# Normalising A through DRAM and GpSimd, and k's transpose ahead of C's, in a fused Nystromformer and GLU kernel

## Chip, cores, metric

One core of one Trainium2 chip. The metric is the device time of that core in microseconds (us), the median of several executions. Most executions of one kernel lie within 0.3 to 1.5% of each other; a few fall in a slower state at a lower granted TensorE clock and are left out of ratios, but not of medians. "TensorE" and PE are the same engine, so are VectorE and DVE, ScalarE and ACT, GpSimd and POOL, SyncE and SP.

## The reference, cut

```python
# q, k, v: [8 batches, 8 heads, 576, 64] fp32; m = 32 landmarks (means over 18 rows)
def sm(a, b): ...                       # softmax(scale * a @ b.T) over the last axis
A  = sm(q, k_lm)                        # 576 x 32
Bm = sm(q_lm, k_lm)                     # 32 x 32
C  = sm(q_lm, k)                        # 32 x 576
Z  = Bm.T / (norm_1(Bm) * norm_inf(Bm) + 1e-6)
for _ in range(6): Z = 2*Z - Z @ Bm @ Z
attn = A @ Z @ C @ v
x   = attn as [4608, 512]
out = (sigmoid(x @ w_gate) * (x @ w_val)) @ w_out      # d_ff = 1536
```

## The kernel before

The program lays eight batches over each other. It carries a small model of the chip and a scheduler: every step says which data it needs, the model says when they will be there, and the scheduler emits instructions in that planned time. The order on each engine is fixed when the kernel is built; on the chip an engine takes its instructions in that order and waits wherever data are not there yet. The last stage of the FFN (`op`) serves as filler while other data are awaited. Names that recur below: `sa`, `sl` and `bs` are the scores for A, C and B; `sm` the row sums of A; `ct` is C transposed and `cv` the product C V; `n`, `s` and `pn` are matmuls on the way to Z; `gp` and `vp` are the FFN's gate and value products, which VectorE joins to `ht` (a "gate"), and `op` is the output product, copied out to `ob`.

How the model plans DMA, from which the order follows:

```python
def turn(self, src, dst):               # DMA transpose
    start = max(self.free["pe"], self.free["sp"], self.landed.get(src.name, 0.0))
    busy = 0.026 * elements / 2048
    self.free["sp"] = start + busy
    end = self.free["sp"] + (3.0 if self.free["dma"] > start else 2.5)
    ...                                 # landed[dst] = end
def swap(self, src, dst):               # the small copies of s4, below
    ...
    end = max(self.free["sp"], self.free["dma"]) + 2.5
SLACK, LAG, FILL = 0.02, 20, 1.0        # of the scheduler: how far it fills ahead, and so on
```

Front of a batch: k and q are turned by DMA, GpSimd sums them to landmarks, halves are exchanged by DMA, and `klm`, `bq` come out.

```python
for what in ("k", "q") if b >= TURN else ():            # TURN = 3
    ...
    turned[what] = turn(t, ..., n, ...)                 # kT, qT on the SP queue
for what in ("k", "q"):
    ...
    pool.tensor_add(out=s1, in0=t[:, :, 0:P6], in1=t[:, :, P6:2 * P6])       # 768 columns
    pool.tensor_add(out=s2, in0=s1, in1=t[:, :, 2 * P6:3 * P6])              # 768 columns
    if b >= SWAP and what == "k" and b < B - 1:         # SWAP = 3
        load(b + 1, "k"); load(b + 1, "q")
    pool.tensor_add(out=s3, ...); pool.tensor_add(out=s4, ...)               # 256 columns each
...                                                     # s4 halves swapped by DMA on SP
pool.tensor_add(out=klm, in0=hls["k"], in1=other["k"])
for c in range(2):
    pool.tensor_add(out=bq[r, :, m * c:m * c + m], in0=hls["q"][r], in1=other["q"][r])
```

Middle of a batch: scores for C (`sl`) and B (`bs`) need `bq`; C's rows `cl` are turned by DMA to `ct`; `cv` = C V follows. DVE spreads B into block diagonals, each product with two sources in SBUF.

```python
ct = sb.tile([128, 2 * NC, 128], BF16, name=f"ct_{b}", tag="ct", bufs=1)
turn(ct, ct, cl, cl.rearrange("p g c x -> p (g c x)"))
turned_c[b] = ()
...
dve.tensor_mul(out=dst[:, g], in0=blk, in1=src[...])    # bdT from Bt, later bd from Bc
ce = dve.tensor_scalar_add(out=ce, in0=cc, scalar1=1e-6)
def late_value():
    yield need(ct, v_landed[0], banks=1, tile='cv')     # 48 small matmuls cv <- vn, ct
```

A's normalisation, and which front may start:

```python
def norm(b):                    # per batch: 10 sm, DVE reciprocal and split, rtp,
    ...                         # 10 rb, and 4 products on DVE
    an = sb.tile([128, 2, S], BF16, name=f"an_{b}", tag="an", bufs=3)
    dve.tensor_mul(out=an[:, g, n0:n0 + nn], in0=aexp[:, g, n0:n0 + nn], in1=rb)
def fronts():
    for b in range(B):
        yield ... made(mid_of, b - 2)
        if b > TURN: yield made(turned_c, b - 1)        # C's transpose first
        yield from front(b)
```

The softmax here doesn't subtract the row's maximum and nothing guards it: scores larger than these inputs give would overflow.

## Time and profile before

| | before |
|---|---|
| time, median | 271.88 us (271.79 to 272.63) |
| span in the trace | 269.7 us |
| busy: PE, DVE, ACT, POOL | 260.1, 193.3, 159.4, 96.2 us |
| granted TensorE clock | 0.998 |

The lines on TensorE are shown in the prediction. The SP queue around 120 us (start, time to issue, what): C's transpose goes out ahead of k's.

```profile
DMA to landing us min/median/max: 3.8/4.6/5.1
```

DVE spreads B (`bdT`, two instructions, 0.36 us) at 121.5; GpSimd's first sum of k for batch 5 begins at 126.9, well after it.

```profile
121.53 0.36 DVE L153 TENSOR_TENSOR bdT<-blk,Bt 128x128 bf16<-128x128 bf16 x2
```
```profile
126.92 1.64 POOL L153 TENSOR_TENSOR s_5k<-kT 128x768 f32<-128x768 bf16 x1 [11.31 <-DMA kT<-kn]
```

### The profile page before, as it was taken

The numbers are of one execution on the slowest core, as the hardware profiler recorded it, in microseconds if no ns is written. First come the engines' busy times: TensorE is split into PE (matmuls) and PEld (weight loads), VectorE is DVE, ScalarE is ACT, GpSimd is POOL, SyncE is SP. The second block draws the span as 40 slices with busy tenths as digits, with TensorE's granted clock in tenths as the row PEclk, the third lists the DMA queues.
The fourth block names the chain that finished last, engine by engine and source line by source line (L and its number), as shares of the span: only waits on it lengthen the run. The fifth ranks groups of instructions, "written<-read, shape, count | busy, mean of one in ns | idle before, by whom it ended". The sixth has DMA issues, their size and how long they took to land.

```text
span 269.7 us, 8019 instructions
## 1 busy us (share of the span) xinstructions
PE 260.1 (96%) x3089; PEld 167.0 (62%) x3123; DVE 193.3 (72%) x551; ACT 159.4 (59%) x413; POOL 96.2 (36%) x107
## 2 busy tenths in 40 slices
PE   8999999999999999999999999999999999999994
PEld 5877777757664666556646665556636664665443
DVE  4566888976899788948986778848968786963111
ACT  3663876866647754876477655875368643964001
POOL 8523231960874039511953078212922000000000
PEclk9999999999999999999999999999999999999999
DMA  6999999999795998889794989589530413101433
GB/s 94 193 206 205 205 206 206 205 203 172 141 194 115 204 170 121 181 135 199 141 221 72 182 157 203 129 139 199 124 90 12 97 41 80 41 0 41 117 103 92
DMA packets 62645, 38.00 MB, mean 141 GB/s; under 512 B 33552, under 2 KB 58128, under 8 KB 62608
## 3 DMA queue, kind: packets, MB, share of 16 engines
q0 software_dynamic: 23600, 18.88, 47.0%
q1 hardware_dynamic: 38896, 18.52, 31.4%
q8 instruction: 24, 0.39, 0.6%
q14 instruction: 13, 0.11, 0.1%
q10 hardware_dynamic: 112, 0.10, 0.1%
HBM read 37.75 MB, written 9.44 MB: 175 GB/s over the span
## 4 chain that ended last, share of the span: by engine, by line
PE 93%; ACT 2%; issue 2%; POOL 1%; DVE 0%; POOLq 0%; ACTq 0%
PE op L247 34%; PE gp L247 18%; PE vp L247 18%; PE idle_ps L247 3%; PE pn L247 2%; PE cv L247 2%; PE rb L247 2%; PE sc L247 1%; PE sa L247 1%; PE tp_q L252 1%; PE up_1g L247 1%; PE up_0g L247 1%; PE up_2g L247 1%; PE tp_k L252 1%; PE up_1v L247 1%
## 5 line engine op out<-in xcount | busy, mean ns | idle before, releaser
L247 PE MATMUL op<-wo_sb,ht 128*128 128x512 bf16 (+1 forms) x410 | 109.4, 373 | 2.1 <-issue 1.1
L153 ACT ACTIVATE th<-gp 128x288 bf16<-128x288 f32 x192 | 76.7, 415 | 48.4 <-PE gp L247 36.7
L153 DVE SCALAR_TENSOR_TENSOR ht<-th,vp 128x288 bf16<-128x288 bf16 x192 | 82.0, 448 | 21.9 <-ACT th L153 17.2
L247 PE MATMUL gp<-an,U 128*128 128x288 bf16 x384 | 78.5, 286 | 0.3
L247 PE MATMUL vp<-an,V 128*128 128x288 bf16 x384 | 78.4, 286 | 0.0
L247 PEld LDWEIGHTS <-ht 128*128 128x128 bf16 x444 | 39.9, 98 | 26.7 <-issue 5.8
L247 PEld LDWEIGHTS <-U 128*128 128x128 bf16 x384 | 35.9, 98 | 27.3 <-issue 2.5
L247 PEld LDWEIGHTS <-V 128*128 128x128 bf16 x384 | 37.5, 98 | 9.7 <-issue 0.2
L153 ACT ACTIVATE ob<-op 128x512 f32<-128x512 f32 (+1 forms) x31 | 18.2, 587 | 29.6 <-PE op L247 24.2
L153 DVE SCALAR_TENSOR_TENSOR sy<-sy,pn 128x384 bf16<-128x384 bf16 x35 | 19.2, 548 | 2.3 <-PE pn L247 1.9
L153 DVE TENSOR_SCALAR ob<-op 128x512 f32<-128x512 f32 (+2 forms) x7 | 4.2, 596 | 17.3 <-PE op L247 17.3
L247 PE MATMUL idle_ps<-idle_w 128*128 128x256 bf16 x86 | 14.8, 308 | 1.2 <-DVE idle_w L297 1.2
L247 PE MATMUL pn<-sy 128*128 128x192 bf16 (+1 forms) x84 | 13.1, 237 | 0.4 <-ACT kT L153 0.3
L153 DVE TENSOR_TENSOR an<-aexp,rb 128x384 bf16<-128x384 bf16 (+1 forms) x32 | 12.4, 446 | 0.3 <-PE rb L247 0.3
L247 PEld LDWEIGHTS <-sy 128*128 128x128 bf16 x88 | 8.1, 97 | 6.2 <-DVE sy L153 2.8
L153 ACT ACTIVATE aexp<-sa 128x288 bf16<-128x288 f32 x32 | 10.7, 418 | 1.5 <-PE sa L247 1.1
L247 PEld LDWEIGHTS <-idle_w 128*128 128x128 bf16 x86 | 8.5, 109 | 3.3 <-DVE idle_w L297 1.2
L247 PEld LDWEIGHTS <-WT 64*32 64x32 bf16 x384 | 3.8, 89 | 9.1 <-issue 6.6
L270 POOL DMA_DIRECT2D kn<-in_k_dram x9 | 7.0, 779 | 4.6 <-DMA wg_sb<-in_moe_w_gate_dram 2.1
L153 DVE CAST U<-up_0g 128x512 bf16<-128x512 f32 x8 | 5.5, 690 | 4.1 <-PE up_0g L247 4.1
L270 POOL DMA_DIRECT2D vn<-in_v_dram x8 | 6.3, 789 | 5.3 <-PE gp L247 4.5
L270 POOL DMA_DIRECT2D qn<-in_q_dram x9 | 6.8, 753 | 4.0 <-PE sm L247 2.2
(201 smaller groups left out, 349.7 us busy)
## 6 DMA issues: line engine op xcount, KB each, us to landing
vn<-in_v_dram POOLq DMA_DIRECT2D x8, 576.0 KB, 9.4
kn<-in_k_dram POOLq DMA_DIRECT2D x7, 576.0 KB, 8.1
qn<-in_q_dram POOLq DMA_DIRECT2D x7, 576.0 KB, 10.6
out_dram<-ob SPq DMA_DIRECT2D x53, 64.0 KB, 3.0
out_dram<-ob SPq DMA_DIRECT2D x17, 192.0 KB, 2.3
out_dram<-ob SPq DMA_DIRECT2D x18, 128.0 KB, 2.4
wg_sb<-in_moe_w_gate_dram POOLq DMA_DIRECT2D x3, 512.0 KB, 19.7
wv_sb<-in_moe_w_val_dram POOLq DMA_DIRECT2D x3, 512.0 KB, 21.0
```

Of the source, the lines that this page charges most:

```text
L153: f(**kw)
L247: nc.tensor.matmul(**kw)
L252: nc.tensor.transpose(**kw)
L270: nc.gpsimd.dma_start(out=t[:, hs], in_=src[b, hs].rearrange("h (p c) d -> p h (c d)", p=P6))
```

## The change

Intent: take matmuls from TensorE and products from DVE. **W**: for batches 3 to 6 the row sums of A come from 8 tiled matmuls, DVE takes reciprocals, they are written to DRAM and read back by four broadcast reads issued behind each other, and GpSimd multiplies A in place. **K**: from batch 4 on, k's transpose and sums go ahead of C's transpose, so that GpSimd has done them before the products come; for this the fronts start by another rule, and the loads of the next k and q are issued later. **Rest**: products are made in place (`aexp` has three buffers, `an` goes away, the last `y` has one buffer).

```diff
+    def widen(self, src, dst, n=1):                    # the model's plan of write and reads
+        start = max(self.free["pe"], self.free["sp"], self.landed.get(src.name, 0.0), ...)
+        self.free["sp"] = start + 0.5 * n
+        end = self.free["sp"] + 3.2
...
-        for what in ("k", "q") if b >= TURN else ():
+        for what in ("k", "q") if TURN <= b <= SWAP else ():
+            yield from turned_by_dma(what)
         for what in ("k", "q"):
+            if b > SWAP:
+                if what == "q":
+                    yield made(turned_c, b - 1)         # only q waits for C's transpose
+                yield from turned_by_dma(what)
+                if what == "q" and b < B - 1:
+                    load(b + 1, "k")
...
-            if b >= SWAP and what == "k" and b < B - 1:
+            if b == SWAP and what == "k":
                 load(b + 1, "k")
+                load(b + 1, "q")
+            elif b > SWAP and what == "q" and b < B - 1:
                 load(b + 1, "q")
...
-        aexp = sb.tile([128, 2, S], BF16, name=f"aexp_{b}", tag="aexp", bufs=2)
+        aexp = sb.tile([128, 2, S], BF16, name=f"aexp_{b}", tag="aexp", bufs=3)
...
+    def wide_norm(b, aexp):                            # WIDE = 3 <= b < B - 1
+        for c in range(2):
+            for j in range(4):
+                mm(out=sm[32 * j:32 * j + 32, :], lhsT=pairs[0][:, c], rhs=aexp[...], ...)
+        for x in range(2):
+            at = dve.reciprocal(out=ra[:, half], in_=sm[:, half])
+        nc.sync.dma_start(out=far..., in_=ra)
+        for i in range(NP):
+            nc.sync.dma_start(out=wide[32 * i:32 * i + 32],
+                in_=far[:, :, i, 0].rearrange("g w x -> (g w) x").partition_broadcast(32))
+        for j in range(4):
+            pool.tensor_mul(out=part, in0=part, in1=wide[:, j])
...
-        an = sb.tile([128, 2, S], BF16, name=f"an_{b}", tag="an", bufs=3)
+        an = aexp
-            ... name=f"y_{b}_{it + 1}", tag=f"y{last}", bufs=2)
+            ... name=f"y_{b}_{it + 1}", tag=f"y{last}", bufs=1 if last else 2)
...
-            if b > TURN:
+            if TURN < b <= SWAP:
                 yield made(turned_c, b - 1)
             yield from front(b)
```

More of the change, by code (lines that the diff above doesn't have):

```diff
@@ L140, in swap @@
         self.used[src.name] = self.used[dst.name] = self.landed[dst.name] = end
+    def widen(self, src, dst, n=1):
+        start = max(self.free["pe"], self.free["sp"], self.landed.get(src.name, 0.0),
+                    self.waits.get(dst.name, 0.0))
+        self.free["sp"] = start + 0.5 * n
+        end = self.free["sp"] + 3.2
+        self.used[src.name] = self.used[dst.name] = self.landed[dst.name] = end
 class Timed:
@@ L209 @@
     ITERS = 6
-    DEFER = {"bs": 1.0, "sl": 1.0, "sa": 3.0, "cv": 0.5, "up": 0.0}
+    DEFER = {"bs": 1.0, "sl": 1.0, "sa": 3.0, "cv": 0.5, "up": 0.0, "sm": 1.0}
     LEAD, FIRST, ORDER = 100.0, (2,), ('k2', 'q2', 'o0', 'o1', 'o2', 'v2', 'k3', 'q3', 'v3')
@@ L217 @@
     SWAP = 3
+    WIDE, QT, pairs = 3, S // 4, []
     consts = ctx.enter_context(tc.tile_pool(name="consts", bufs=1))
@@ L222 @@
     sb = ctx.enter_context(tc.tile_pool(name="sb", bufs=2))
+    away = ctx.enter_context(tc.tile_pool(name="away", bufs=1, space=bass.MemoryType.DRAM))
     ps = ctx.enter_context(tc.tile_pool(name="ps", bufs=3, space=bass.MemoryType.PSUM))
@@ L410, in front, with turned_by_dma @@
         ends = {}
-        for what in ("k", "q") if b >= TURN else ():
+        def turned_by_dma(what):
             yield made(nat, (what, b))
@@ L716, in mid @@
             value_of[b] = late_value
+    def wide_norm(b, aexp):
+        if b == WIDE:
+            pairs.append(consts.tile([128, 2, 32], BF16, name="pairs"))
+            nc.vector.memset(pairs[0], 0.0)
+            to = pairs[0].rearrange("p c (i u d) -> p c i u d", u=4, d=2)
+            for c in range(2):
+                dve.tensor_copy(out=to[:, c, :, :, c], in_=blk0_[:, :, None].to_broadcast([128, NP, 4]))
+        yield need(aexp, banks=1, tile='sm')
+        sm = bank([128, QT], FP32, f"sm_{b}")
+        for c in range(2):
+            for j in range(4):
+                o = (j % 2) * HF + c * QT
+                mm(
+                    out=sm[32 * j:32 * j + 32, :], lhsT=pairs[0][:, c],
+                    rhs=aexp[:, j // 2, o:o + QT], start=(c == 0), stop=(c == 1))
+        ra = sb.tile([128, QT], FP32, name=f"ra_{b}", tag="ra", bufs=1)
+        for x in range(2):
+            half = slice(x * QT // 2, (x + 1) * QT // 2)
+            at = dve.reciprocal(out=ra[:, half], in_=sm[:, half])
+            yield need(at + (0.3 if x == 0 else 0.0))
+        far = away.tile([2, 2, NP, 4, HF], FP32, name=f"far_{b}", tag="far", bufs=2)
+        nc.sync.dma_start(out=far.rearrange("g w i u (c x) -> (g w i u c) x", c=2), in_=ra)
+        model.widen(ra, far)
+        wide = sb.tile([128, 4, HF], FP32, name=f"rw_{b}", tag="rw", bufs=1)
+        for i in range(NP):
+            nc.sync.dma_start(
+                out=wide[32 * i:32 * i + 32],
+                in_=far[:, :, i, 0].rearrange("g w x -> (g w) x").partition_broadcast(32))
+        model.widen(far, wide, NP)
+        yield need(wide)
+        for j in range(4):
+            part = aexp[:, j // 2, (j % 2) * HF:(j % 2 + 1) * HF]
+            pool.tensor_mul(out=part, in0=part, in1=wide[:, j])
+        an_of[b] = aexp
     def norm(b):
         aexp = norm_of.pop(b)
+        if WIDE <= b < B - 1:
+            yield from wide_norm(b, aexp)
+            return
         yield need(aexp, banks=1)
@@ L783, in first_newton @@
             last = it == ITERS - 1
-            n = sb.tile([128, 2, 2, D] if last else [128, 2, D], BF16, name=f"y_{b}_{it + 1}", tag=f"y{last}", bufs=2)
+            n = sb.tile([128, 2, 2, D] if last else [128, 2, D], BF16, name=f"y_{b}_{it + 1}", tag=f"y{last}", bufs=1 if last else 2)
             model.by_part.add(n.name)
```

## The prediction

> **What bounds the kernel now.** I read the page first: engines, slices, chain.
>
> ```profile
> PE 260.1 (96%) x3089; PEld 167.0 (62%) x3123; DVE 193.3 (72%) x551; ACT 159.4 (59%) x413; POOL 96.2 (36%) x107
> PE   8999999999999999999999999999999999999994
> PEclk9999999999999999999999999999999999999999
> PE 93%; ACT 2%; issue 2%; POOL 1%; DVE 0%; POOLq 0%; ACTq 0%
> ```
>
> TensorE is busy in every slice, at full granted clock, and 93% of the chain that ends last is TensorE itself. Since a pipelined matmul can look busy while it waits, I then read the table of windows for the steady part, where batches 3 to 6 are normalised.
>
> ```profile
> 124.00:130.00 6.00, 5.84 (x108) 4.00 (x108) 4.83 (x18) 3.51 (x10) 3.00 (x2) 1.00 0.99 197
> 130.00:136.00 6.00, 5.95 (x51) 4.03 (x51) 5.77 (x17) 2.41 (x7) 5.83 (x7) 1.00 0.81 127
> 160.00:166.00 6.00, 5.95 (x52) 4.11 (x52) 5.70 (x17) 2.44 (x6) 5.83 (x6) 1.00 0.99 158
> 178.00:184.00 6.00, 5.95 (x43) 3.93 (x42) 3.35 (x14) 4.50 (x18) 0.00 (x0) 1.00 1.25 221
> ```
>
> The columns are the length, then PE, its weight loads, DVE, ACT, POOL, then clock, DMA share and GB/s. PE has 5.84 to 5.95 of 6 us; DVE looks near full where it normalises (5.77), but its records overlap (two gates stand 0.365 us apart though each is recorded as 0.447), so it has room. To see whether PE's busy time is work or disguised waiting, I went through the timeline start by start:
>
> ```profile
> 125.18 0.41 PE L247 MATMUL vp<-an,V 128*128 128x288 bf16 x2
> 125.52 0.44 PE L247 MATMUL sa<-qT,klm 64*32 64x288 bf16 x16
> ...
> 127.47 0.41 PE L247 MATMUL sm<-blk,aexp 128*128 128x4 bf16 x10
> 127.74 0.59 PE L247 MATMUL op<-wo_sb,ht 128*128 128x512 bf16 x2
> ...
> 129.25 0.22 PE L252 MATMUL rtp<-ident,rhl 128*80 128x128 bf16 x1
> 129.31 0.41 PE L247 MATMUL gp<-an,U 128*128 128x288 bf16 x2
> ...
> 130.40 0.68 PE L247 MATMUL rb<-rt,sel 80*128 80x128 bf16 x10
> 130.91 0.60 PE L247 MATMUL op<-wo_sb,ht 128*128 128x512 bf16 x2
> ```
>
> What an instruction costs is the distance to the next start, not its recorded length: a pair of gp is 0.245 us, a pair of op 0.43. When I lay these distances on the built order of matmuls, nothing of weight is left over from batch 3 on: the largest excess between two neighbouring gp is 0.2 us. So PE has no stall there to be freed; only the matmuls themselves can become fewer, and anything that arrives late is a pure loss.
>
> **What the Trainium skill says.** "TensorEngine Tiling (Array Packing)", Tiling Modes, Key Properties: changing the tiling mode drains the array. The trace agrees and gives the size: from vp at 125.18 two matmuls of 0.1225 end at 125.42, sa starts at 125.52; all eleven entries from vp into a tiled group show 0.093 to 0.094 us. "GPSIMD Engine Reference", 3.1 Elementwise: about 2.6 cycles an element for two inputs at 1.2 GHz, 2.17 ns; the trace has 1.64 us for 768 elements, 2.13 ns, so it agrees. "DMA: Bandwidth & Descriptors", Anatomy of one DMA: some 2 us are fixed in each transfer, most of it the receipt; the trace has 1.9 us to landing for 32 KB outputs and 2.3 for 192 KB, so it agrees. "Perfetto Trace Analysis", Identifying the Most-Contended Engine, warns that matmul busy share is no measure of headroom; that is why I counted starts.
>
> **The change, part by part.** All four steps concern batches 3, 4, 5 and 6 only.
>
> 1. Removed on PE, per batch: ten sm matmuls, 0.27 us (127.47 to 127.74); one transpose rtp, 0.07 (56 to 87 ns over the batches); ten rb, 0.51 (130.40 to 130.91). Sum 0.85, four times 3.4 us.
>
> 2. Added on PE, per batch: eight matmuls of 144 columns into four strips of 32 columns. Four strips run beside each other, as in the up groups, where sixteen of 512 columns take about 0.45 us net of drains. So two rounds of 144 columns: 2 x 144/512 x 0.213 = 0.12 us, four times 0.5 us.
>
> 3. Drains. In the built order the changes between tiled and untiled mode rise from 88 to 104. Three of the four new sm groups stand alone (two changes each), the one of batch 5 joins the cv group; the rest comes from groups that used to stand together and are now apart (sa from cv in batches 2, 5 and 7, a split of sl in batch 5, bs from up in batch 1), because the order has shifted. 16 x 0.094 = 1.5 us lost. One more idle matmul at the start: 0.1 us.
>
> Sum on PE: -3.4 + 0.5 + 1.5 + 0.1 = **-1.3 us**. This is the whole gain that can reach the end.
>
> 4. DVE: the four products go away.
>
> ```profile
> L153 DVE TENSOR_TENSOR an<-aexp,rb x32: 344/446/553, 24.2 to 223.0; 128x384 bf16<-128x384 bf16 x16, 128x192 bf16<-128x192 bf16 x16
> L153 DVE RECIPROCAL sm<-sm x8: 405/408/417, 21.9 to 218.9; 128x40 f32<-128x40 f32 x8
> ```
>
> Per batch 4 x 0.446 = 1.8 us, the reciprocal 0.41, two splits of 0.2 and the rt copy 0.2; added are two reciprocals of 72 columns, an estimate of 0.6 us each from 0.41 at 40 columns. So about 1.6 us less a batch, 6 in all. It lies beside PE and is worth nothing directly. GpSimd gets 4 products of 288 elements, 4 x (0.1 + 288 x 2.13 ns) = 2.8 us a batch; it is 36% busy, so this fits in total. Its order is what counts.
>
> 5. The new chain. The old one ran PE, DVE, PE, DVE, PE, DVE in about 5 us (sm at 127.5, last product at about 132.5). The new one: sm, two reciprocals (1.2), a write to DRAM (2.3 to 3), four broadcast reads, issued one behind another at 0.55 each (the two halves of s_4k take 1.1 on the queue) and moving 590 KB at the 200 GB/s the page shows (3 us) plus 2 us fixed, then 2.8 on GpSimd: 12 to 14 us, more where q and k loads share the DMA engines. The built order has put first use of the result far back: laid out by the starts above, sm to first gp grows from 13 to 15 us to 27, 20, 26 and 17 us. PE fills this with op matmuls, which are no extra work. So the chain itself fits in every batch.
>
> 6. k ahead of C's transpose. GpSimd stands idle for k's transpose in every batch:
>
> ```profile
> POOL s_4k L153 <- DMA kT<-kn: 12.9, 1, 12.9
> POOL s_6k L153 <- DMA kT<-kn: 11.5, 1, 11.5
> POOL s_5k L153 <- DMA kT<-kn: 11.3, 1, 11.3
> ```
>
> The change starts it some 10 us earlier and thereby makes room on GpSimd for the products. PE did not wait for these sums, so it gains nothing directly.
>
> **Rivals.**
> (a) A late product stalls PE. For it: in GpSimd's order the products of batch 3 stand behind the sums of kT_5, those of batch 5 behind kT_7. From the transpose's issue it is 5.9 us to landing, then 4.8 us of sums, then 2.2 us to the third product, which the first gp needs: 13 us, and the built order leaves about 15 us between that place and the first gp. Slack is 2 us in batches 3 and 5, 3 or more elsewhere. A wait behind broadcast traffic or output writes could eat it: 0 to 2 us each, which would give 271.5 to 274. Against it: before, the same planner left PE no stall.
> (b) DVE or ACT becomes the bound. Because op tiles are run in advance while the product is awaited, the gp and vp come in denser runs later; each pair of pairs needs a tanh and a gate per 0.49 us of PE, and a gate takes 0.365. Against it: around 203 us the kernel before runs eight such units in a row at 0.488 without a gap, and DVE has 6 us less to do. If it came, 1 to 2 us lost: about 272.5.
> (c) Outputs and swaps are held up on the one queue behind the wait for the DRAM write (some 2.5 us, four times). Output buffers are three and a tile comes every 6 us, so it should hide: no effect.
> (d) The gain is larger, about 268 to 269: it would need a stall before that DVE or GpSimd caused. I found none after batch 3, and the first 60 us are hardly touched.
>
> **Range and chances.** -1.3 on PE, and for (a) and (b) an expected loss of 0.6, gives 271.88 - 0.7, **271.2 us**. Low end: the whole gain and some of (d), 269.6. High end: two stalls of (a) and a bit of (b), 273.4. 2% is 5.4 us: faster would need four times the PE work that is saved net, 0.03; slower needs a stall of nearly 7 us, which only a broadcast far slower than thought could make, 0.04; within 2%, 0.93.
>
> **What would show it.** Busy PE should fall by 2 to 4 us of its records; the new sm groups should stand 0.12 us plus two drains of 0.094 from their neighbours; rb and rtp should number half; DVE busy should fall by some 6 to 8 us, POOL rise by about 11. The waits should show s_5k to s_7k waiting less for kT, and no wait of PE of over 1 us for the products in batches 4 and 6. The read from DRAM should land in 4 to 7 us. I am wrong if PE shows a gap of several us before the first gp of batch 3 or 5, if a product on GpSimd takes well over 0.8 us, or if PE falls by more than 3 us in the span.

## More of the kernel before

```profile
119.13 1.88 SPq L384 DMA_TRANSPOSE ct<-cl  x1
121.11 3.52 SPq L384 DMA_TRANSPOSE kT<-kn  x1
```

The second is the view of the tile `ct`: time from issue to landing of its five transposes.

## The result, and the profile after

Ratios here and below are the mean time of one kernel's fast runs over the mean of the other's in the same rounds, so not quite the ratio of the medians that are quoted.

| | before | after |
|---|---|---|
| median (lowest to highest) | 271.95 us (271.79 to 272.63) | 284.62 us (281.54 to 286.61) |
| ratio | | 1.042, 95% interval 1.034 to 1.051 |
| span of the profiled run, clock | 269.7 us, 0.998 | 279.3 us, 0.991 |

The change makes the kernel slower by 4.2%. The profiled run of the changed kernel is its fastest, 9.7 us behind the kernel before. From its page: engines, PE and clock in 40 slices, and the chain that ended last.

```profile
PE 265.1 (95%) x3072; PEld 164.3 (59%) x3072; DVE 194.6 (70%) x534; ACT 158.6 (57%) x409; POOL 107.0 (38%) x123
PE   7899999999998899987999999998999999999994
PEclk9999999999999999997999999999999999999998
PE 56%; DMA 25%; POOL 9%; DVE 4%; issue 2%; SPq 1%; ACT 1%; POOLq 0%; DVEq 0%; ACTq 0%
```

Slices below 9 have appeared in PE's row, the clock dips, and 25% of the chain are now DMA and 9% GpSimd, where before 93% were TensorE. So TensorE waits. The timeline of PE at the deepest place (start, length, what, how many, and in brackets the idle time and what ended it):

```profile
124.07 0.44 PE L258 MATMUL sa<-qT,klm 64*32 64x288 bf16 x16
127.16 0.56 PE L258 MATMUL cv<-vn,ct 96*32 96x64 bf16 x48 [2.65 <-DMA ct<-cl]
127.65 3.99 PE L258 MATMUL op<-wo_sb,ht 128*128 128x512 bf16 x10
131.57 0.31 PE L258 MATMUL sm<-aexp,pairs 128*32 128x144 bf16 x8
```

TensorE stands 2.65 us for C's transpose of batch 4. Before, the same pair `sa`, `cv` follows without a gap (125.52, then 125.89). The wait costs a second time: the ten `op` after it take 3.92 us to the next start, where ten take 2.15 at 0.215 each. The table of windows tells why; the last numbers are clock, DMA share and GB/s:

```profile
127.70:131.00 3.30, 3.30 (x10) 1.13 (x9) 0.60 (x2) 0.00 (x0) 3.14 (x6) 0.50 0.94 237
```

The granted clock is half. This one place costs 2.65 + 1.8 = 4.4 us. The SP queue shows what was ahead of C's transpose, and the view of the tile `ct` how long its transposes took to land:

```profile
115.66 2.88 SPq L395 DMA_TRANSPOSE kT<-kn  x1
119.15 1.72 SPq L1022 DMA_DIRECT2D out_dram<-ob  x4
121.39 1.57 SPq L395 DMA_TRANSPOSE ct<-cl  x1
```
```profile
DMA to landing us min/median/max: 3.7/5.7/6.1
```

Its source was ready at 118.1 by the trace (the last `cl` ends there); k's transpose and four outputs were ahead of it in the queue, it went out at 121.39 and landed at 127.12. The other transposes land later too: k's took 5.9 us in the median before, 8.7 after.

A second kind of loss stands at 93 to 96 us. DVE, then GpSimd, then PE:

```profile
93.47 0.74 DVE L161 TENSOR_SCALAR ce<-cc 128x2 f32<-128x2 f32 x1
95.05 1.07 DVE L161 TENSOR_TENSOR bd<-blk,Bc 128x128 bf16<-128x128 bf16 x2
```
```profile
92.54 1.64 POOL L161 TENSOR_TENSOR s_4k<-kT 128x768 f32<-128x768 bf16 x1 [6.76 <-DMA kT<-kn]
94.26 1.64 POOL L161 TENSOR_TENSOR s_4k<-s_4k,kT 128x768 f32<-128x768 f32 x1
```
```profile
96.54 0.64 PE L258 MATMUL sa<-qT,klm 64*32 64x288 bf16 x9 [0.70 <-DVE ht L161]
```

`ce` is an addition on two columns, some 0.17 us elsewhere; here it takes 0.74 and ends at 94.21, just after GpSimd's sum of k ends at 94.18. The first of the two `bd` takes 0.94 us in place of 0.22 and ends at 95.98, just after the second sum ends at 95.90. The gates behind them are late, and TensorE waits 0.70 us for one.

TensorE's other waits of over 0.4 us from batch 1 on: 0.84 and 0.46 us for `bq` at 84 to 85, 0.45 for `bq` at 181, about 0.5 for `bdT` at 186 (by the distances of starts), 1.07 for `ct` of batch 6 at 191. With 2.65, 0.70 and the 1.8 of half clock these are 8.5 us, of the 9.6 us by which the spans of the profiled runs differ. Batch 3, where `bq` is awaited at 84 to 85, is one that K does not touch.

### The profile page after: what moved, and what is told of

Read it like the earlier page. It is cut to its first block, busy times and chain, and to the rows that moved or that the text cites. A ratio compares the mean times of both kernels' runs of the same rounds, so it can differ in the third digit from the quotient of the medians.

```text
span 279.3 us, 8001 instructions
## 1 busy us (share of the span) xinstructions
PE 265.1 (95%) x3072; PEld 164.3 (59%) x3072; DVE 194.6 (70%) x534; ACT 158.6 (57%) x409; POOL 107.0 (38%) x123
## 4 chain that ended last, share of the span: by engine, by line
PE 56%; DMA 25%; POOL 9%; DVE 4%; issue 2%; SPq 1%; ACT 1%; POOLq 0%; DVEq 0%; ACTq 0%
PE op L258 21%; PE gp L258 10%; PE vp L258 9%; DMA ct<-cl 4%; DMA qT<-qn 4%; DMA kT<-kn 4%; DMA far<-ra 3%; DMA qn<-in_q_dram 3%; DMA rw<-far 2%; PE idle_ps L258 2%; POOL bq L161 2%; DMA s_6q<-s_6q 2%; POOL s_6q L161 2%; POOL s_3q L161 2%; DMA s_5q<-s_5q 2%
## 5 line engine op out<-in xcount | busy, mean ns | idle before, releaser
L161 DVE SCALAR_TENSOR_TENSOR ht<-th,vp 128x288 bf16<-128x288 bf16 x192 | 81.0, 447 | 10.6 <-ACT th L161 8.1
L258 PE MATMUL gp<-aexp,U 128*128 128x288 bf16 x384 | 78.5, 286 | 0.0
L258 PE MATMUL vp<-aexp,V 128*128 128x288 bf16 x384 | 78.4, 286 | 0.0
L258 PEld LDWEIGHTS <-ht 128*128 128x128 bf16 x444 | 40.5, 99 | 38.0 <-issue 8.7
L161 ACT ACTIVATE ob<-op 128x512 f32<-128x512 f32 (+1 forms) x23 | 13.4, 584 | 32.6 <-PE op L258 29.8
L161 DVE TENSOR_SCALAR ob<-op 128x512 f32<-128x512 f32 (+2 forms) x15 | 9.7, 646 | 30.1 <-PE op L258 30.0
L161 POOL TENSOR_TENSOR aexp<-aexp,rw 128x288 bf16<-128x288 bf16 x16 | 11.2, 736 | 15.5 <-DMA rw<-far 8.4
L161 ACT ACTIVATE aexp<-sa 128x288 bf16<-128x288 f32 x32 | 10.8, 418 | 0.7 <-PE sa L258 0.3
L161 DVE TENSOR_SCALAR sy<-cv,rcs,rc 128x64 bf16<-128x64 f32 x14 | 4.2, 339 | 8.0 <-PE cv L258 7.6
L161 ACT ACTIVATE cl<-sl 128x288 bf16<-128x288 f32 x20 | 8.0, 410 | 2.3 <-PE sl L258 2.1
## 6 DMA issues: line engine op xcount, KB each, us to landing
vn<-in_v_dram POOLq DMA_DIRECT2D x8, 576.0 KB, 10.3
```

Source lines behind the costliest of these rows:

```text
L161: f(**kw)
L258: nc.tensor.matmul(**kw)
```

## The experiments

Each run was timed in rounds beside the kernel before on the same chip (its median was 271.7 to 273.0 there). "Order" is the built order of instructions on all five engines.

| run | what | median us | ratio to before, 95% |
|---|---|---|---|
| e1_k_only | K and rest | 278.39 | 1.021 [1.016, 1.026] |
| e2_wide_only | W and rest | 277.99 | 1.019 [1.013, 1.025] |
| e7_inplace_only | rest alone | 277.69 | 1.020 [1.015, 1.025] |
| e3_no_wait | change, reads don't wait for the write | 282.70 | 1.034 [1.028, 1.041] |
| e4_quarter | change, a quarter of the reading | 283.23 | 1.035 [1.027, 1.043] |
| e5_ct_act | change, C's transpose on ScalarE's queue | 305.95 | 1.124 [1.117, 1.131] |
| e6_late_cv | change, C's landing planned 4 us later | 282.28 | 1.033 [1.027, 1.039] |
| e8_wide_late | W and rest, reads planned later | 275.16 | 1.013 [1.006, 1.020] |
| e10_both_late | change, both planned later | 285.76 | 1.041 [1.032, 1.051] |
| e15_both_lag | change, another order | 281.89 | 1.037 [1.031, 1.043] |
| e17_wide_robust | e8 with swaps planned later too | 282.12 | 1.037 [1.030, 1.044] |
| e13_inplace_order | rest alone, in the order of before | 272.26 | 0.999 [0.993, 1.005] |
| e11_lag | before, another order | 278.20 | 1.020 [1.013, 1.027] |
| e12_slack | before, nearly the same order | 272.09 | 0.998 [0.992, 1.003] |
| e14_light_loads | change, its order, an eighth of the loads | 274.79 | 1.013 [1.005, 1.020] |
| e18_lag_light | e11, its order, an eighth of the loads | 272.47 | 1.001 [0.997, 1.005] |
| e19_before_light | before, its order, an eighth of the loads | 271.89 | 1.000 [0.994, 1.005] |
| e20_short_sums | e14, its order, short sums of k | 271.44 | 0.999 [0.994, 1.004] |

### The parts apart

K without W, W without K, and neither:

```diff
# e1_k_only
-    WIDE, QT, pairs = 3, S // 4, []
+    WIDE, QT, pairs = B, S // 4, []
# e2_wide_only: the fronts, transposes and loads as before
-        for what in ("k", "q") if TURN <= b <= SWAP else ():
+        for what in ("k", "q") if b >= TURN else ():
-            if TURN < b <= SWAP:
+            if b > TURN:
...
# e7_inplace_only: both edits
```

> The changed kernel with the old normalisation in all batches (no DRAM round trip, no GpSimd products), k's transpose and sums ahead of C's transpose kept. Its order of matmuls costs 0.7 us more than that of the kernel before by the starts of the trace. Theory K (k's transpose, now ahead of C's in the one queue, makes C's land late, cv stalls TensorE and the clock drops): a stall of cv of 1 to 3 us in at least one batch, time 274 to 278. Rival W (the DRAM round trip of the reciprocals fills or blocks the queue and delays what stands behind it): no stall here, time 272 to 273.5. Rival P (late products): the same as W.

> The changed kernel with its DRAM round trip and GpSimd products, but the fronts as before: C's transpose first, then k's and q's. By the starts, its order costs 1.1 us less than before. Theory K: no wait of cv for C's transpose, time 270.5 to 273. Rival W: the stalls stay, time 277 or more. Rival P: a gap before the first gp of a batch, time 274 or more.

> Neither of the two parts: what is left of the change are the products written in place, three buffers for aexp and one for the last y. By the starts its order costs 0.3 us more than before. If the two parts hold the whole loss: 271.5 to 273. If the wait of bs in batch 3 for bq (1.4 to 1.9 us in all runs of the changed order so far but one) belongs to this rest: 273 to 275.

All three lose 5.4 to 6.1 us: 278.4, 278.0 and 277.7. The expectation of e7 was missed in both its forms, and that of theory K in e2 as well. So 277.7 is reached with none of W or K, with buffers and an in-place product alone, and each part alone adds 0.3 to 0.7, within the intervals. Both together add 6.9 to it. The traces differ in what TensorE waits for: in e1 and e7 `cv` waits for `ct`, up to 1.7 and 2.1 us. In e2 the rival (a) of the prediction came true; PE's timeline:

```profile
142.99 4.05 PE L258 MATMUL op<-wo_sb,ht 128*128 128x512 bf16 x18
148.94 0.28 PE L258 MATMUL gp<-aexp,U 128*128 128x288 bf16 x1 [1.90 <-POOL aexp L161]
```

No filler stands between the 18 `op` and the first `gp`, which waits 1.90 us for GpSimd's product. In the whole change it never does: the third product of batches 3 to 6 is done 1.2, 3.6, 4.3 and 3.8 us ahead of the first `gp`.

### The chain through DRAM by itself

```diff
# e3_no_wait: reads take rows of v, so they need not wait for the write (wrong output on purpose)
-                in_=far[:, :, i, 0].rearrange("g w x -> (g w) x").partition_broadcast(32))
+                in_=v[b, 0:4].rearrange("h s d -> h (s d)")[:, i * HF:(i + 1) * HF].partition_broadcast(32))
# e4_quarter: each read brings one row of four, and all products use it
-                out=wide[32 * i:32 * i + 32], in_=far[:, :, i, 0]....partition_broadcast(32))
+                out=wide[32 * i:32 * i + 32, 0:1], in_=far[0, 0:1, i, 0].partition_broadcast(32))
-            pool.tensor_mul(out=part, in0=part, in1=wide[:, j])
+            pool.tensor_mul(out=part, in0=part, in1=wide[:, 0])
```

> The changed kernel in exactly the same order, but the four broadcast reads take rows of v in DRAM in place of the reciprocals just written, so that the queue does not wait for the write (the output is wrong on purpose). Bytes and pieces of the reads stay. Theory K: cv still waits about 2 to 3 us in batch 4, time within 3 us of the changed kernel's, 279 to 286. Rival W in its form of a blocked queue (10.4 us of waiting for the write over four batches): at most 276.

> The changed kernel in the same order, but each broadcast read brings one of its four rows, so a quarter of the bytes (output wrong on purpose); the wait for the write stays. Theory K: cv still waits in batch 4, since its transpose stands behind k's, time 278 to 285. Rival W in its form of traffic (590 KB a batch beside the loads of q, k and v): at most 276, and the swap of q and C's transpose land 3 us or more earlier.

Both keep the order, and both give back little: 282.7 and 283.2 against 284.6, with overlapping intervals. In e3's trace `cv` still waits for `ct`, 1.84 and 3.03 us. Neither the wait of the reads for the write nor the read traffic is the main cost. (e4's output passed as correct: the row sums are so alike that one row's reciprocals serve for the others.)

### C's transpose

```diff
# e5_ct_act
-            turn(ct, ct, cl, cl.rearrange("p g c x -> p (g c x)"))
+            nc.scalar.dma_start_transpose(out=ct, in_=cl.rearrange("p g c x -> p (g c x)"))
+            model.turn(cl, ct)
# e6_late_cv: the plan puts cv 4 us later
+            model.landed[ct.name] += 4.0
             turned_c[b] = ()
```

> The changed kernel in exactly the same order on every engine, but C's transpose is issued by ScalarE in place of SyncE, so it stands no more behind k's transpose and the output writes in one queue. Theory K (C's transpose is late because of what stands ahead of it): cv waits for C's transpose by under 0.5 us in all batches, the stretch from 90 to 130 us keeps its clock, time 275 to 280 (the products and the early waits stay). Rival: C's transpose is late because the DMA engines are full with loads; then it lands as late as in the changed kernel and the time stays at 281 to 286.

> The changed kernel, but the kernel's own plan takes C's transpose to land 4 us later, so cv is placed later in TensorE's order (5 us more between sl and cv in batch 4) and nothing else is touched by hand. If the loss comes from matmuls placed before their data lands, cv does not wait and the time is 275 to 279; if it comes from the added work itself, the time stays above 281.

e5 could not answer its question. On ScalarE's queue the transpose had to wait until k's had landed (at 128.36), and ScalarE with it:

```profile
128.50 1.46 ACTq L623 DMA_TRANSPOSE ct<-cl  x1
130.01 0.53 ACT L161 ACTIVATE Bc<-E,rr 128x32 bf16<-128x32 f32 x2 [7.76 <-issue]
```

TensorE then waited 3.8 to 7.0 us for `Bc` in four batches. All that it shows is that the transpose, once issued, landed in 3.7 to 3.8 us, at times when next to no loads moved (their queue had 3% and 6% of the DMA engines' time in the two of these stretches that were looked up).

e6 took away the waits for `ct` (6 to 8 us of room), and the time fell by 2.3 us only, within the intervals: TensorE now waited 3.4 and 1.1 us for a GpSimd product, 1.5 for `bq` and 1.1 for `bdT`. The wait had moved.

### Room in the plan

```diff
# e8_wide_late: e2 with
-        end = self.free["sp"] + 3.2
+        end = self.free["sp"] + (3.2 if n == 1 else 8.5)
# e10_both_late: the changed kernel with e6's edit and this one
# e15_both_lag: the changed kernel with
-    SLACK, LAG, FILL = 0.02, 20, 1.0
+    SLACK, LAG, FILL = 0.02, 22, 1.0
# e17_wide_robust: e8, and in swap
-        end = max(self.free["sp"], self.free["dma"]) + 2.5
+        end = max(self.free["sp"], self.free["dma"]) + 5.0
```

> The round trip alone (fronts as before), but the plan takes the broadcast reads to land 8.5 us after their last issue in place of 3.2 (7 to 8.9 us were seen in two of the batches of the round trip alone). If late products are its loss: TensorE does not wait for GpSimd's products, time 271 to 274.5. If the loss is in the traffic or the drains: 276 or more, as without the later plan.

> The whole change, planned with C's transpose landing 4 us later and the broadcast reads 5.3 us later than its own plan takes. If the loss is a matter of matmuls placed before their data lands, neither cv nor the products are waited for by over 0.5 us, and it falls to 273 to 277, below both the change (281.5 to 286.6) and the later cv alone (280.4 to 282.8). If waits merely move to the landmarks' swaps (bs for bq), 277 to 281.

> The whole change with a lag of 22 in place of 20. By the starts its order costs the same 251.2 us and the places of gp are the same to 1 us up to batch 6. If the loss depends on the exact order, the time may fall anywhere from 275 to 287; if it is the change's own work or the structure of its order (op in advance, then products and C's transpose needed at once): 281 to 286.6 again.

> The round trip alone, fronts as before, the broadcast reads planned 5.3 us later and the landmarks' swaps 2.5 us later. If room for landings is what is missing: bs waits for bq by under 0.5 us from batch 3 on (in the run with the later reads alone it lost 0.5 to 1.6 in three batches), time 270.5 to 274; otherwise 275 to 279 as the other orders.

Only e8 seems to have helped: with landings planned as the trace has them, W alone comes to 275.2 in place of 278.0, though its interval (1.006 to 1.020) overlaps that of e2, and it is still above the kernel before. e10 was a miss: the waits went from `ct` and the products to `bq`, 4.8 and 3.4 us. e17 was a miss as well: more room for the swaps gave 282.1, with new waits for `ct` (1.7 us) and for ScalarE's `Bc` (2.1 us). A more generous plan is just another order, and may meet late data elsewhere.

### The same work in another order

```diff
# e11_lag: the kernel before with
-    SLACK, LAG, FILL = 0.02, 20, 1.0
+    SLACK, LAG, FILL = 0.02, 22, 1.0
# e12_slack: the kernel before with
+    SLACK, LAG, FILL = 0.03, 20, 1.0
# e13_inplace_order: in-place product and buffers of the change; the model is told of the
# product under a stand-in name, so that all five engines keep the order of before
+        an = aexp
+        plan = Planned(f"an_{b}")
+                model.run("dve", [plan], [aexp, rb], 0.065 + nn / 960.0, 0.12)
```

> The kernel before with the products written in place and the buffer counts of the change, while its plan does not learn of it: the order of instructions on all five engines is exactly that of the kernel before. Theory N (what the rest of the change costs, 5.4 us, is its other order alone, in which data lands after TensorE asks for it): 271.5 to 273. If writing in place or the single buffer costs time itself: 275 or more.

> The kernel before with nothing changed but one constant of its plan, the lag between the two main streams (22 units in place of 20); 590 rows of TensorE's order differ and the work is the same. Theory N (the order of the kernel before is one that happens to leave every landing 1 us or more of room, and others do not): 274 to 279, with waits of bs for bq or of cv for C's transpose. Rival: the order is not delicate, and the loss is in what the change does: 271.5 to 273.5.

> The kernel before with another constant of its plan, the slack of 0.03 in place of 0.02 us; only 37 rows of TensorE's order differ, and the places of sl, cv and gp move by 0.1 us. Theory N asks only that landings keep their room, so 271.5 to 273: a control that a changed build in itself costs nothing.

e13: the in-place product and the buffers cost nothing, 0.999. So what e7 lost is its order. e11 does the work of the kernel before in another order, with no instruction more or less (by the traces four copies go from VectorE to ScalarE and one the other way), and loses 5.2 us; in e12 37 rows of TensorE's order differ and nothing is lost. PE's timeline of e11:

```profile
156.22 0.44 PE L247 MATMUL sa<-qT,klm 64*32 64x288 bf16 x16
159.59 0.56 PE L247 MATMUL cv<-vn,ct 96*32 96x64 bf16 x48 [2.92 <-DMA ct<-cl]
```

C's transpose of that batch took 9.7 us to land. From its landing to `cv`, in batches 3 to 7, the kernel before has 2.6, 2.1, 1.6, 2.2, 1.3 us of room; the changed kernel 0.7, 0, 4.0, 0, 5.7; e7 1.5, 0, 0, 0, 1.6; e11 1.5, 0, 0, 2.8, 4.8 (0 is a wait). The order of before is one in which everything lands in time.

### Where the lateness comes from

Loads of q, k and v run at those places. These runs keep the order of every engine and shrink the loads of batches 4 to 7 to one head of eight, into tiles that hold older data (wrong output):

```diff
+            ls = hs if b < 4 else slice(0, 1)
             nc.gpsimd.dma_start(
-                out=t[:, hs], in_=src[b, hs].rearrange("h (p c) d -> p h (c d)", p=P6))
+                out=t[:, ls], in_=src[b, ls].rearrange("h (p c) d -> p h (c d)", p=P6))
```

> The changed kernel, the same order on every engine, but the loads of q, k and v from batch 4 on bring one head of eight and go into the tiles of batches 2 and 3 (output wrong on purpose). If transposes, swaps and broadcast reads land late because they share the DMA engines with these loads: C's transpose lands in about 4 us, k's in about 5, the broadcast reads in 5, cv does not wait in batches 4 and 6, time 272 to 277. If the lateness comes from the queue's own order (k's transpose ahead of C's) or from the work: 280 to 286 as the changed kernel.

> The kernel before with a lag of 22, loads of q, k and v cut to an eighth from batch 4 on, order the same on every engine as with the lag alone (output wrong on purpose). If the loads make the landings late: cv does not wait in batches 4 and 5, time 272 to 274 in place of 276.3 to 279.7. Waits in batch 3 stay, since its loads are whole.

> Control for the two runs with light loads: the kernel before, same order on all engines, with the loads of q, k and v of batches 4 to 7 cut to one head of eight (wrong output on purpose). Theory N (in the new orders TensorE waits for data that land late because the loads share the DMA engines; in the order of before nothing lands late) expects no gain here, because there is nothing to give back: 271 to 272 us, within 0.3% of the kernel before. The rival that the light loads simply make any order faster (less power, fewer conflicts in memory, GpSimd freed sooner) expects several us less, 265 to 268, as in the changed kernel (10 us) and the order with the other lag (5.5 us).

e18, PE's timeline at the place of e11's wait:

```profile
155.08 0.44 PE L247 MATMUL sa<-qT,klm 64*32 64x288 bf16 x16
155.45 0.55 PE L247 MATMUL cv<-vn,ct 96*32 96x64 bf16 x48
```

The wait is gone, the longest landing of `ct` falls from 9.7 to 5.2 us, and with it the whole loss: 278.2 to 272.5. In the changed kernel with light loads (e14) `ct` lands within 3.7 to 4.2 us, the clock is 1.00, and 9.8 of 12.7 us come back. The control e19 gains nothing (1.000): light loads don't speed up an order in which nothing is late. So these losses are data that land late beside the loads. (Light loads also take GpSimd 0.54 in place of 0.79 us each to issue; by e19 this alone gains nothing.) It is not the place in the queue by itself: in e14 C's transpose of batch 4 still stands behind k's and four outputs and goes out 3.3 us after its source is ready, as in the changed kernel, and `cv` finds it landed by 0.36 us. How the loads stretch a landing is not shown. In e11's 9.7 us, all queues moved 172 GB/s up to 153.5, but from 153.5 to 158.3 only 51, with 0.04 MB of loads: for half of the time the transpose stood while little was moved.

e14 still lost 3 us. In its trace three matmuls `s` wait for DVE's `bdT`, 0.97, 1.22 and 0.84 us. PE, DVE and GpSimd at the middle one:

```profile
120.45 0.23 PE L258 MATMUL s<-bdT 128*128 128x128 bf16 x1 [1.22 <-DVE bdT L161]
```
```profile
118.55 1.84 DVE L161 TENSOR_TENSOR bdT<-blk,Bt 128x128 bf16<-128x128 bf16 x2
```
```profile
118.67 1.64 POOL L161 TENSOR_TENSOR s_5k<-kT 128x768 f32<-128x768 bf16 x1 [6.53 <-DMA kT<-kn]
```

The first `bdT` had begun ahead of the sum; the second began at 118.69, in it, and lasted 1.70 us, to 120.39, 0.08 after the sum's end. The Trainium skill, "SBUF — State Buffer", section "SBUF: two separate sides", says that VectorE and GpSimd share a pair of ports as an exclusive lock: a VectorE instruction with two sources in SBUF and a GpSimd instruction that reads SBUF don't run together, nor does a VectorE instruction in a two-port mode beside one of GpSimd's; the later one waits for the whole of the earlier. The trace agrees in all ten such places of this run after the start-up and in all eight of the changed kernel's: the DVE instruction begins while one of GpSimd's runs and ends within 0.1 us of that one's end (in six of the eight a sum or a product, in two the issue of a load). Adding up what DVE's instructions take beyond the usual length of their form gives 1.0 us before, 4.4 after, 9.5 in e14, and 2.2 and 0.2 with K and with W alone. The last run shortens GpSimd's sums of k and nothing else:

```diff
# e20_short_sums: e14, for k of batches 4 to 7 (the model is told the old lengths; wrong on purpose)
-            pool.tensor_add(out=s1, in0=t[:, :, 0:P6], in1=t[:, :, P6:2 * P6])
+            nc.gpsimd.tensor_add(out=s1[:, 0:1], in0=t[:, 0:1, 0:P6], in1=t[:, 0:1, P6:2 * P6])
...                                # s2 alike; s3 and s4 read head 0 for all heads
```

> The changed kernel with light loads, same order on every engine, with one more edit: GpSimd's two big sums of k for batches 4 to 7 take one head of eight (96 columns in place of 768; the two small sums spread that head; wrong output on purpose). Read from the traces after the earlier runs: with light loads three matmuls s still wait for DVE's bdT, 0.97 + 1.22 + 0.84 = 3.0 us, and each of those bdT lasts 1.4 to 1.7 us in place of 0.22 and ends within 0.1 us of the end of GpSimd's big sum of k that ran beside it; DVE's instructions of this kind are too long by 9.5 us in all there, by 4.4 in the changed kernel, by 1.0 in the kernel before. Theory L (a DVE instruction with two sources in SBUF and a GpSimd instruction shut each other out, and the change puts k's sums where DVE spreads B) expects the three waits to vanish, DVE's excess to fall from 9.5 to under 4 us, and the time to fall from 274.8 to about 272 us. The rival (the 3 us that are left belong to the order or to other late data, and bdT's length is a record that costs nothing) expects 274.5 to 275.

271.44 us, ratio to the kernel before 0.999: the 3 us are gone, as the theory of the lock has it. (The shorter sums also finish the landmarks sooner, but e14 had no wait for `bq` to lose by it.) At the same place (DVE, GpSimd):

```profile
121.27 0.53 DVE L161 TENSOR_TENSOR bdT<-blk,Bt 128x128 bf16<-128x128 bf16 x2
```
```profile
121.32 0.40 POOL L479 TENSOR_TENSOR s_5k<-kT 128x96 f32<-128x96 bf16 x1 [5.99 <-DMA kT<-kn]
```

Of the three waits for `bdT` none of 0.3 us or more is left in batches 4 to 7; one of 1.0 us stands in batch 3, whose sums were not shortened. DVE's excess fell from 9.5 to 5.6 us, less than the "under 4" that I had expected.

No version that was run beats the kernel before; e12 and e13 equal it.

## Why the prediction was wrong, point by point

**The bound, and steps 1 to 3 (TensorE's work).** Right. `rb` and `rtp` number half, the new `sm` groups stand some 0.24 us from the next start (less one drain of 0.094 this leaves 0.15, where I had 0.12), the changes of tiling mode rise from 88 to 104 in the traces too, and the usual distances, laid on the two orders, differ by 1.1 us (for e2's order) to 1.4 us (re-laid on the changed kernel's own trace), where I had 1.3. Busy PE was to fall by 2 to 4 us and rose by 5.0, but the trace before lacks 34 of the 444 `op` records, so that this sign could not be read. With both losses taken away (e20) the kernel comes out at the level of before; so small a gain can't be told from nothing there (0.994 to 1.004).

**Step 4 (DVE and GpSimd).** GpSimd rose by 10.8 us as said, a product takes 0.736 us, a reciprocal of 72 columns 0.60. From the groups:

```profile
L161 POOL TENSOR_TENSOR aexp<-aexp,rw 128x288 bf16<-128x288 bf16 x16 | 11.2, 736 | 15.5 <-DMA rw<-far 8.4
```

DVE busy was to fall by 6 to 8 us and rose by 1.3. The products did go (7 us) and the longer reciprocals came (3), but the scheduler moved eight of the copies of `op` from ScalarE to DVE (`ob`, 4.2 to 9.7 us), and instructions held by the lock add 3.4. I had counted instructions and not asked what beside them GpSimd would be doing.

**Step 5 (the new chain).** Nearly right: the reads land in 2.6 to 7.0 us, where I had 4 to 7, the write in 1.7 to 5.7 (median 2.3), and the chain fits in every batch. Rival (a) is not the cause in the whole change; it is in e2 and e6. (The skill's 2 us that the prediction set beside two landings stand under the path of GpSimd's queue; the landings read, 1.9 and 2.3 us, are of SyncE's.)

**Step 6 failed**, with the argument that stood against rival (a), "before, the same planner left PE no stall". Step 6 has k's transpose start 10 us earlier, which makes room on GpSimd, and TensorE gain nothing by it; a cost isn't considered. That holds for the plan only. By the traces k's transposes of batches 4 to 7 went out 3.6 to 7.7 us earlier and landed only 2.5 to 5.8 us earlier. C's transpose then stood behind k's and four outputs and landed late beside the loads (2.65 and 1.07 us of waits, and a half clock behind the first), and k's sums come to lie exactly where DVE spreads B, and hold it. What the place in the queue costs by itself stays open: e7, with C's transpose first, has waits for it of 0.96 and 2.12 us too, and e14 keeps the place without them. Rival (c), "no effect" of a queue held up, asked only what the outputs need, not the small transposes and swaps behind them; e3 takes its wait for the write away and gives back 1.9 us, within the intervals, so that more than this is not shown against it.

**The premise under all steps failed first**: that a new built order is as free of late landings as the old, so that -1.3 us is "the whole gain that can reach the end". I laid distances of starts on the new order and so assumed it. The runs show what the premise is worth: the rest alone, without W or K, costs 2.0% in its own order (e7) and nothing in the order of before (e13), and the work of the kernel before in another order costs 2.0% (e11). Hence the range, 269.6 to 273.4, held only the costs of work and none of order; a chance of 0.04 for slower was far too small.

What is shown: late landings beside the loads cost the changed kernel most of its loss (e14 with its control e19); the exclusion of DVE by GpSimd costs 3 us of what is left there (e20). What is not: how the two share the 12.7 us with full loads, since with light loads k's sums come at other times and DVE is held longer (9.5 us in place of 4.4). In the changed kernel as it is I read about 1.2 us of direct waits from the lock (0.70 and 0.5). That both parts together cost 6.9 us more than the rest alone fits both causes, and the four orders of the whole change that were tried give 281.9 to 285.8, but no run takes it apart. The reading of e7 and e11 as "order" rests on e13, e18 and e19.

## What to carry to other kernels

In a statically ordered kernel that runs without a stall, first build the same work in another order and time it: what that costs (here 2%) is the noise in which any rearrangement is judged, and it is paid by a change even if its own work is cheaper. Before moving a transfer ahead in a queue, list what stands behind it and how much room that has at its first use; here it was 1.3 to 2.6 us, and with full loads beside it a landing took 9.7 us in place of 5.2. Before moving work to GpSimd or in time on it, look at which DVE instructions with two sources in SBUF run at that moment; each can be held for the whole length of GpSimd's, here up to 1.70 us in place of 0.22.

## What the Trainium skill lacked or had wrong

- "SBUF — State Buffer" has the lock right, and the prediction should have read it. It also lists copies and `tensor_scalar` among the instructions that can be held, and `ce`, one of these, took 0.74 us in the changed kernel and 1.50 in e14 in place of 0.17, ending within 0.03 us of GpSimd's sum.
- "DMA: Bandwidth & Descriptors" gives a fixed 2 us and a rate for one transfer, and says that transfers of all queues interleave on the same engines, but has no time for how far a landing stretches by it: the same transpose (`ct`) lands in 3.7 to 5.2 us beside light loads and in up to 9.7 beside full ones; k's in 4.9 to 10.3.
- "TensorE: Matmul & The Clock Gate" has the clock fall to half after an idle window of about 3.4 us. Here a wait of 2.65 us was enough for 3.4 us at half clock (0.50 from 127.7 to 131.0), while one of 3.03 us in e3 left the clock at 1.00.
- "TensorEngine Tiling (Array Packing)" says that a mode change drains the array and gives no size: 0.093 to 0.094 us here.
- No page says that the order alone, of the same work, can cost as much as it did: 273.0 against 278.2 us in the same rounds (e11, with five copies on another engine).
